# The head of an adaLN attention and GLU block: modulation weights in two pieces, K and Q passes interleaved, LayerNorm divided differently, planner constants refitted

## The chip, the cores and the metric

One core of a Trainium2 chip runs the whole program. The metric is the device time of one execution in microseconds. Before the change the median of 3 runs is 815.4 us (813.98 to 816.16). A profiled execution is recorded beside these runs; its span, from the program's first to its last recorded work, is 812.1 us. Engines are named as the profile names them: PE (TensorE, matrix products), PEld (its weight loads), DVE (VectorE), ACT (ScalarE), POOL (GpSimd), SP (SyncE, which here only issues DMAs).

## What is computed

```python
mod = silu(c) @ w_mod                      # 6 vectors of 640: sa, ca, ga, sb, cb, gb
h = layernorm(x) * (1 + ca) + sa           # x: 2048 x 640
q, k, v = split(h @ wqkv)                  # 32 heads of 20
p = softmax(q @ k.T * 20**-0.5)            # per head 2048 x 2048
x = x + ga * ((p @ v) @ wo)
h = layernorm(x) * (1 + cb) + sb
x = x + gb * (((h @ w_gate) * (h @ w_up)) @ w_down)   # 640 -> 1536 -> 640
```

All inputs and outputs are bf16. The largest piece of elementwise work is the softmax's exponential over 32 x 2048 x 2048 scores.

## The kernel before

**A planner in Python.** The kernel does not write its instruction order by hand. Each operation is a `Task` (L34) with an engine, a planned duration, dependences and a priority; `Sched` (L118) simulates the engines and lays tasks out in a fixed order for each engine, and `emit_program` (L322) writes that order with semaphore waits. At run time each engine works its list strictly in order: an instruction that waits holds all behind it on the same engine. `steal` (L272) lets the planner give an evacuation (a copy out of PSUM) that was meant for DVE to ACT. The constants at the top steer the plan: `QUADS` (L433), `HEADG` (L440), `LN_ACT` (L496), `GATE_F`, `STAGE` (L511 to 549, overrides by item) and others.

**Head.** One DMA each brings c (SP queue), token tiles 0 and 1 of x (`x00`, SP) and tiles 2 and 3 (`x01`, ACT queue), modulation vector 0 (`wm0`, sa, SP) and vector 1 (`wm1`, ca, ACT queue), each of 640x640 (`load_wm`, L801). The SP queue then waits for the first LayerNorm instruction (`ln_mark`) and issues the first half of wk, x of token chunk 1, the first half of wq, and so on (`load_rest`). A token chunk has 512 tokens, four tiles of 128. `col_round` (L927) multiplies one modulation vector's weights with silu(c), 25 matmuls per vector, into columns that an operation on DVE puts into `mcol`. `ln1` (L965) normalizes the four tiles of a chunk: by BN_STATS on DVE (L1012 to L1021), or, for tiles in `LN_ACT`, by two passes on ACT with accumulation (L975, L978); both with a power on POOL (L1021) and a normalization on DVE. `hT_rounds` (L1047) transposes the normalized tiles on PE, 128x128 each, by feature block of 128 columns (L1068, four tiles for each block), and evacuates each block with the modulation applied (ACT L1074, DVE L1076), after both modulation vectors. `kq_round` (L1102) then computes 4 heads of K (20 matmuls, L1107, evacuated by L1120/L1121), and of Q (L1127/L1128); `packed_round` (L1165) does so for other heads; `v_round` (L1248) computes V in quarter tiles (L911, L1260/L1261). Where PE has nothing, `do_fill` (L2343) issues matmuls without use (L2355 and L2357) that keep it active. `SCb` (L1344) and `load_wm(3/4)` (L1340) prepare the other modulation vectors.

**Attention.** The scores are computed transposed in PSUM, in units of 128 keys x 512 columns (L1448). Most units are exponentiated on ACT (L1484, into PP), in groups of 2 units (128x1024); from group `HEADG` on groups of 3 (128x1536) alternate with groups of 2. Some sets of four units, `QUADS` of them in each item, go to DVE instead, which forms the exponential with integer operations (L1508 into DB, then L1540, L1545, L1548 into DSS). PE multiplies both with V (L2005). The 40 items are 5 query chunks (512, 512, 512, 256, 256 rows) times 8 sets of 4 heads. The rest of the work (wo, the second LayerNorm, the GLU and w_down) of a chunk is spread over the items of the next.

**Tail.** What is left when the last exponential ends: the last PV products, wo, LayerNorm 2 (transposes L1763, evacuation h2Tc L1770 on ACT) and the GLU of the last 256 rows (L907, L911), and the output DMA.

Of the kernel before, what the change touches and what calls it, by code (L numbers as in the profile page):

```python
# [27 lines left out]
STEAL_END = 66197.894  # L28
STEAL_GAP = 200
# [292 lines left out]
def emit_program(nc, sched, nsem_dma=56):  # L322
# [83 lines left out]
    with nc.Block() as block:  # L406
# [20 lines left out]
        def _(e):  # L427
# [5 lines left out]
QUADS = ((0, 4, 3, 3, 3, 3, 4, 4),  # L433
# [6 lines left out]
HEADG = 580  # L440
# [5 lines left out]
LN2T = 0.6  # L446
# [4 lines left out]
XBACK = 1  # L451
# [3 lines left out]
TPRIO = 0.75  # L455
# [4 lines left out]
HEAD_OUT = 2  # L460
NPS = 4
TS_4X, TT_2X = 600.0, 1145.0
WM_GATE = 9
# [9 lines left out]
PVMIN, PVMAX, PVCAP = 2, 7, 13  # L473
PV0 = 0
V_PARTS = [[0, 4], [4, 8]]
V_L1 = 0.2
TAILX = 1
PASSDEP = 0
# [3 lines left out]
PASS_TC = (0, 1, 2, 3)  # L482
HT0_SPLIT = 0
PREEMPT = 0.0
PRE_M = 0.3
PV0N = 1
GATE_F = (0.468, 0.693, 0.969, 0.732, 1.0)
# [8 lines left out]
LN_ACT = [1, 3, 5, 7]  # L496
# [4 lines left out]
HT_L = 0.25  # L501
V_L = 0.221
LATE_A = 2.065
LATE_L = 1.418
LATEQ = (3,)
LATEQ_A = 2
# [6 lines left out]
    1: {"HOLD": 91, "D_LATE": 10, "PVMAX": 7},  # L513
    2: {"DL": 0.376, "D_LATE": 17},
    3: {"STEAL_GAP": 200, "PVMAX": 5, "FILL_MIN": 4781.051, "X_LATE": 38.763},
    5: {"EAGER": 7, "D_RES": 27, "PVCAP": 8},
    6: {"PVCAP": 12, "FILL_MIN": 4102.43, "D_LATE": 12, "PVMIN": 2},
    7: {"DL": 0.501, "PVCAP": 8, "PVTOL": 347},
    10: {"PVMAX": 8, "X_LATE": -27.967, "EAGER": 11, "D_LATE": 9},
    11: {"EAGER": 11, "DL": 0.443, "X_LATE": -8.435, "FILL_MIN": 4364.854, "PVTOL": 245, "HOLD": 134, "PVMAX": 9, "PVCAP": 13},  # L520
    12: {"FILL_MIN": 4969.105, "D_LATE": 7, "STEAL_GAP": 194.93, "X_LATE": -138.337, "DL": 0.459},
    13: {"DL": 0.417, "D_RES": 10, "HOLD": 84, "PVMAX": 6},
    14: {"D_LATE": 14, "D_RES": 22, "FILL_MIN": 4272.896, "EAGER": 10, "X_LATE": -52.696, "STEAL_GAP": 200},
    15: {"X_LATE": -15.741, "FILL_MIN": 4338.164, "HOLD": 175, "EAGER": 13},
    16: {"FILL_MIN": 3909.78, "D_RES": 55, "HOLD": 133, "PVCAP": 11},
    17: {"DL": 0.465, "D_LATE": 17, "PVMAX": 9, "PVMIN": 2, "STEAL_GAP": 195.663},
    18: {"FILL_MIN": 4326.704, "D_RES": 10},
    19: {"D_LATE": 18, "DL": 0.471, "FILL_MIN": 3976.707},
    20: {"DL": 0.391, "D_LATE": 14, "PVCAP": 13, "FILL_MIN": 5000},
    21: {"D_RES": 10, "PVCAP": 20, "HOLD": 96, "PVMAX": 6, "PVMIN": 2, "D_LATE": 19},  # L530
    22: {"PVMAX": 7, "FILL_MIN": 3913.503, "D_RES": 17, "X_LATE": -76.434, "EAGER": 6, "D_LATE": 16, "PVCAP": 13},
    23: {"PVTOL": 247, "PVMAX": 7, "D_RES": 23},
    24: {"PVCAP": 13, "PVMAX": 7, "PVMIN": 2, "FILL_MIN": 4085.526, "DL": 0.464, "EAGER": 7, "STEAL_GAP": 200, "HOLD": 231},
    25: {"STEAL_GAP": 200, "HOLD": 144, "X_LATE": 22.894, "D_RES": 10, "FILL_MIN": 4068.834, "DL": 0.549, "PVCAP": 15, "D_LATE": 14},
    26: {"D_RES": 15, "X_LATE": -39.384, "PVMAX": 9, "PVCAP": 14, "STEAL_GAP": 200, "DL": 0.411},
    27: {"DL": 0.473, "D_LATE": 6, "PVMAX": 6, "EAGER": 6, "D_RES": 75, "PVTOL": 249, "PVMIN": 2, "X_LATE": -47.659},
    28: {"PVCAP": 13, "HOLD": 166, "X_LATE": 82.94},
    29: {"PVCAP": 14, "EAGER": 5, "PVMAX": 7, "D_RES": 46},
    30: {"X_LATE": -110.495, "PVCAP": 15, "FILL_MIN": 3782.61, "D_LATE": 16, "PVTOL": 292},
    31: {"D_RES": 19, "FILL_MIN": 4905.173, "D_LATE": 15, "PVMIN": 2, "X_LATE": 36.868},  # L540
    32: {"PVMIN": 2, "D_LATE": 17, "D_RES": 78},
    33: {"STEAL_GAP": 199.702, "D_LATE": 18, "PVCAP": 14, "PVMAX": 4, "DL": 0.442, "PVTOL": 353, "D_RES": 17, "PVMIN": 2, "HOLD": 100},
    34: {"X_LATE": 150, "D_LATE": 22, "HOLD": 117},
    35: {"PVMIN": 2, "PVMAX": 8, "FILL_MIN": 4516.564, "STEAL_GAP": 179.748, "X_LATE": -53.091, "HOLD": 151, "D_LATE": 12, "PVCAP": 14},
    36: {"PVMIN": 2, "D_RES": 10, "DL": 0.524, "X_LATE": -6.364, "FILL_MIN": 4156.61, "PVMAX": 8, "HOLD": 33},
    37: {"D_LATE": 12, "PVTOL": 254, "PVCAP": 13, "FILL_MIN": 4699.279},
    38: {"D_RES": 60, "PVMAX": 7, "PVTOL": 450, "HOLD": 67, "D_LATE": 16},
    39: {"FILL_MIN": 3000, "D_LATE": 17, "PVTOL": 258, "X_LATE": -54.236, "PVCAP": 16},
}
XHALF = 1  # L550
STG_G0, STG_G, XC_G = 12, -10, -20
X_LATE = -24.052
# [11 lines left out]
def build_kernel(nc, A_x, A_wqkv, A_wo, B_x, B_w_gate, B_w_up, B_w_down, c, w_mod, out):  # L564
# [70 lines left out]
    mcol = alloc("mcol", [128, 4, KD], F32)  # L635
    st = alloc("st", [128, 4, 12], F32)
# [177 lines left out]
    load_wm(0, wm_a[0], "sp", 0.3)  # L814
    load_wm(1, wm_a[1], "act", 0.4)
    for t, land in ((d_x[0][0], 5000.0), (d_x[0][1], 4100.0), (d_wm[0][0], 9400.0), (d_wm[1][0], 8000.0)):
        t.land = land
    chained = [d_x[0][0], d_x[0][1], d_wm[1][0], d_wm[0][0]]

    def chain(f, *a):  # L820
        deps = [ln_mark[0]]
        tot = 0
        for t in reversed(chained[4:]):
            if tot >= DMA_WINDOW:
                deps = [t]
                break
            tot += t.nbytes
        f(*a, deps)
        return deps

    def load_rest():
        chain(load_w, d_wk, 0, 1, wk_sb, 0, "sp", 0.5)
        chained.append(d_wk[0])
        first2 = [lambda: chain(load_x, 1, 0, "sp", 0.6), lambda: chain(load_w, d_wq, 0, 0, wq_sb, 0, "sp", 0.55 if WQ_FIRST else 0.7)]
        if WQ_FIRST:
            first2.reverse()
        for q, f in enumerate((first2[0], first2[1],
# [126 lines left out]

    def ln1(tc, prio):  # L965
# [3 lines left out]
        for i in range(4):  # L969
            t = tc * 4 + i  # L970
            if t in LN_ACT:
                jx = xn[:, s2, i, :]
                tiny = (lambda f_, d_: dve(75, f_, d_, prio=prio + .1 * i)) if tc < 2 else (
# [6 lines left out]
                if i == 0 and tc == 0:  # L980
# [3 lines left out]
                p2 = pool(570, lambda e, t=t: e.tensor_tensor(rs[:, t:t + 1], sd[:, t:t + 1], mhalf[:, 0:1], ALU.pow),  # L984
                          [q4, p_mh], prio=prio)
# [25 lines left out]
            for hf in range(2):  # L1011
                bns.append(dve(393, lambda e, t=t, i=i, hf=hf: e.bn_stats(  # L1012
                    st[:, i, 6 * hf:6 * hf + 6], x0[:, t, 320 * hf:320 * hf + 320]),
                    [d_x[tc][i // 2], ag_prev.get(i)], prio=prio + .1 * i))
                if t == 0:
                    ln_mark[:] = bns[-1:]
            ag = dve(75, lambda e, t=t, i=i: e.bn_aggr(mv[:, t, :], st[:, i, :]), bns, prio=prio + .1 * i)
            ag_prev[i] = ag
            f1 = lambda e, t=t: e.tensor_scalar(sd[:, t:t + 1], mv[:, t, 1:2], EPS, None, op0=ALU.add)
            p1 = dve(75, f1, [ag], prio=prio + .1 * i) if tc < 2 else pool(220, f1, [ag], prio=prio)  # L1020
            p2 = pool(570, lambda e, t=t: e.tensor_tensor(rs[:, t:t + 1], sd[:, t:t + 1], mhalf[:, 0:1], ALU.pow),  # L1021
                      [p1, p_mh], prio=prio)
            f = lambda e, t=t, i=i: e.tensor_scalar(
# [3 lines left out]
            else:  # L1027
                t_xn[tc].append(dvl(360, f, [p2] + dps, prio=prio + .05 + .1 * i))

    t_hT = {}  # L1030

    def hT_rounds(tc, prio):
# [3 lines left out]
        if tc == 0 and HT0_SPLIT:  # L1036
            bs = [{} for _ in range(KD)]
            prev = None
            for i in range(4):
                for k in range(KD):  # L1040
# [4 lines left out]
                    if i == 0:  # L1045
# [9 lines left out]
                    if i == 3:  # L1055
# [46 lines left out]
    def kq_round(kind, j, tc, prio, gate=0):  # L1102
# [50 lines left out]
        elif tc not in LATEQ:  # L1153
            proj_early.append(r.last)
# [1278 lines left out]
```

## Time and profile before

| what | value |
|---|---|
| median of 3 runs | 815.4 us (813.98 to 816.16) |
| span of the profiled execution | 812.1 us |
| granted PE clock, mean | 1.00 |
| exponentials on ACT (L1484) | 677 of 128x1024 (mean 1126 ns), 98 of 128x1536 (mean 1546 ns) |
| units on DVE (L1508) | 400 (mean 680 ns), 100 chains of DSS operations (705, 688, 1224 ns) |
| first exponential starts | 15.90 us |
| ninth exponential starts | 26.67 us |
| last exponential ends | 779.23 us |
| fill matmuls | 23 of 128x512, 300 of the 32-column kind |

How to read the lines shown below. In the list of groups each line gives a line of the kernel, engine, operation, output and inputs, shapes, the count, busy time in us, mean ns of one, and the idle time of the engine just before them, with what ended it. In the list of waits: who waited for whom, the total in us, how often, and the longest. In the busy time by stage: the stretch, its length, then busy us of PE, PEld, DVE, ACT and POOL with instruction counts, the granted PE clock, the DMA share and GB/s. In the chain and the timeline: start, duration in us, and what ran.

### The profile page before, as it was taken

The numbers are of one execution on the slowest core, as the hardware profiler recorded it, in microseconds if no ns is written. First come the engines' busy times: TensorE is split into PE (matmuls) and PEld (weight loads), VectorE is DVE, ScalarE is ACT, GpSimd is POOL, SyncE is SP. The second block draws the span as 40 slices with busy tenths as digits, with TensorE's granted clock in tenths as the row PEclk, the third lists the DMA queues.
The fourth block names the chain that finished last, engine by engine and source line by source line (L and its number), as shares of the span: only waits on it lengthen the run. The fifth ranks groups of instructions, "written<-read, shape, count | busy, mean of one in ns | idle before, by whom it ended". The sixth has DMA issues, their size and how long they took to land.

```text
span 812.1 us, 28878 instructions
## 1 busy us (share of the span) xinstructions
PE 784.0 (97%) x12493; PEld 305.3 (38%) x12493; DVE 719.8 (89%) x1275; ACT 773.8 (95%) x818; POOL 79.1 (10%) x105
## 2 busy tenths in 40 slices
PE   9999999999999999999999999999889999999998
PEld 4433333322233223233233322233244444554567
DVE  7989999899999999999999999998999886667753
ACT  7899999999999999999999999999999999999942
POOL 3300000020002000000011000000011000001000
DMA  9624211214330244000400222000400146105610
GB/s 314 204 84 105 69 46 37 52 29 124 95 68 25 52 104 134 23 11 22 93 6 6 55 48 61 6 18 23 87 8 22 39 95 139 36 30 130 142 37 17
DMA packets 116445, 54.71 MB, mean 67 GB/s; under 512 B 83915, under 2 KB 116319, under 8 KB 116319
## 3 DMA queue, kind: packets, MB, share of 16 engines
q1 hardware_dynamic: 115391, 51.72, 24.6%
q8 instruction: 99, 1.62, 0.8%
q10 hardware_dynamic: 928, 1.15, 0.4%
q14 instruction: 27, 0.22, 0.1%
HBM read 41.85 MB, written 8.41 MB: 62 GB/s over the span
## 4 chain that ended last, share of the span: by engine, by line
PE 40%; ACT 37%; DVE 15%; issue 7%; DMA 1%; ACTq 0%; DVEq 0%
ACT PP L1484 37%; PE ps_all L911 12%; PE ps_all L1448 12%; PE ps_all L2005 9%; DVE DB L1508 5%; PE ps_all L907 3%; DVE DSS L1545 2%; DVE DSS L1548 2%; DVE DSS L1540 1%; PE ps_all L1171 1%; PE ps_all L1107 1%; DMA wm<-in_w_mod_dram 1%; PE ps_all L1068 1%; DVE wd L1434 1%; DVE gsb L1852 1%
## 5 line engine op out<-in xcount | busy, mean ns | idle before, releaser
L1484 ACT ACTIVATE PP<-ps_all 128x1024 bf16<-128x1024 f32 (+1 forms) x775 | 754.7, 1179 | 4.4 <-PE ps_all L1448 3.0
L1448 PE MATMUL ps_all<-QT,KT 32*128 32x512 bf16 (+1 forms) x2560 | 308.1, 340 | 18.1 <-ACT PP L1484 12.4
L1508 DVE TENSOR_SCALAR DB<-ps_all 128x512 int16<-128x512 f32 x400 | 264.4, 680 | 35.7 <-PE ps_all L1448 34.7
L1448 PEld LDWEIGHTS ps_all<-QT,KT 32*128 32x128 bf16 x2560 | 81.3, 91 | 262.7 <-ACT PP L1484 235.3
L2005 PE MATMUL ps_all<-PP,Vf 128*32 128x512 bf16 (+2 forms) x2084 | 164.2, 343 | 0.4 <-DVE OT L1632 0.4
L1545 DVE TENSOR_TENSOR DSS<-DB,DSS 128x2048 bf16<-128x2048 bf16 x100 | 122.4, 1224 | 0.0
L911 PE MATMUL ps_all<-h2T,stg 128*32 128x512 bf16 (+1 forms) x1740 | 115.9, 345 | 0.9 <-DVE DB L1508 0.2
L1638 POOL TENSOR_TENSOR OTn<-OT,invT 128x512 bf16<-128x512 f32 (+1 forms) x39 | 46.6, 1195 | 598.9 <-DVE invT L1636 598.9
L2005 PEld LDWEIGHTS ps_all<-PP,Vf 128*32 128x32 bf16 (+1 forms) x2084 | 45.9, 93 | 87.5 <-issue 79.8
L2005 PE MATMUL ps_all<-DSS,Vf 128*32 128x512 bf16 (+3 forms) x952 | 77.3, 349 | 0.9 <-DVE DSS L1545 0.5
L1540 DVE TENSOR_SCALAR DSS<-DB 128x2048 int16<-128x2048 int16 x100 | 70.5, 705 | 0.8
L1548 DVE TENSOR_SCALAR DSS<-DB 128x2048 int16<-128x2048 int16 x100 | 68.8, 688 | 0.3 <-PE ps_all L2005 0.3
L911 PE MATMUL ps_all<-wd,hprod 128*32 128x320 bf16 (+1 forms) x1316 | 58.5, 284 | 0.1
L911 PEld LDWEIGHTS ps_all<-h2T,stg 128*32 128x32 bf16 x1740 | 38.9, 95 | 34.6 <-issue 17.6
L911 PEld LDWEIGHTS ps_all<-wd,hprod 128*32 128x32 bf16 x1316 | 31.2, 96 | 16.6 <-issue 7.4
L2005 PEld LDWEIGHTS ps_all<-DSS,Vf 128*32 128x32 bf16 (+1 forms) x952 | 23.9, 95 | 24.4 <-issue 14.1
L911 PE MATMUL ps_all<-wV,hT 128*32 128x320 bf16 (+1 forms) x704 | 32.3, 289 | 0.1
L1171 PE MATMUL ps_all<-hT,wq 128*32 128x512 bf16 x375 | 31.6, 382 | 0.1
L911 PE MATMUL ps_all<-wo,Ocp 128*32 128x320 bf16 (+1 forms) x628 | 28.2, 286 | 0.3
L2357 PE MATMUL ps_all<-ident 128*32 128x512 bf16 x300 | 27.0, 383 | 0.3 <-DVE DB L1508 0.2
L1852 DVE CAST gsb<-ps_all 128x512 bf16<-128x512 f32 x36 | 24.4, 678 | 3.0 <-PE ps_all L911 3.0
L1632 DVE STREAM_TRANSPOSE OT<-ps_all 128x512 f32<-128x512 f32 (+1 forms) x40 | 24.1, 602 | 2.8 <-PE ps_all L2005 2.7
(122 smaller groups left out, 507.0 us busy)
## 6 DMA issues: line engine op xcount, KB each, us to landing
stg<-in_B_w_gate_dram SPq DMA_DIRECT2D x50, 160.0 KB
stg<-in_B_w_up_dram SPq DMA_DIRECT2D x50, 160.0 KB
QT<-q_rows SPq DMA_DIRECT2D x22, 128.0 KB
KT<-k_rows SPq DMA_DIRECT2D x84, 32.0 KB
wm<-in_w_mod_dram SPq DMA_DIRECT2D x3, 800.0 KB
x<-in_A_x_dram SPq DMA_DIRECT2D x7, 320.0 KB
xck<-in_A_x_dram SPq DMA_DIRECT2D x3, 640.0 KB
wd<-in_B_w_down_dram SPq DMA_DIRECT2D x1, 1920.0 KB
```

Of the source, the lines that this page charges most:

```text
L911: return lambda e, b: e.matmul(ps[32 * x:32 * x + 32, b, c0 + o:c0 + o + w], lhs()[:, 32 * x:32 * x + 32], rhs() if w == n else rhs()[:, o ...
L1171: f = [lambda e, b_, k=k, x=x: e.matmul(ps[x:x + min(32, w - x), b_, :], wx[:, k, r0 + x:r0 + min(x + 32, w)], hT[tc][:, k, :], tile_posit ...
L1448: ems.append(lambda e, i=i, kt=kt: e.matmul(dstf()[:, i * u.n:(i + 1) * u.n], KT[32 * u.s:32 * u.s + 32, u.j, kt * 128:(kt + 1) * 128], QT ...
L1484: return e.activation(PPs[g % 2][:, cellp["p"], 0:nu * 512], ps[:, b0:b0 + nu, :].rearrange("p b c -> p (b c)"), AFT.Exp, scale=ESCALE)
L1508: return e.tensor_scalar(DB0[:, st_["slot"], x * 512:(x + 1) * 512], bank(cell["b"]), EBIAS, 0.0, op0=ALU.add, op1=ALU.max)
L1540: return e.tensor_scalar(DSS[:, st_["ss"][0], :], DB0[:, st_["slot"], :], 0x7F, 0x3F00, op0=ALU.bitwise_and, op1=ALU.bitwise_or)
L1545: return e.tensor_tensor(d, DB0[:, st_["slot"], :].bitcast(BF16), d, ALU.mult)
L1548: return e.tensor_scalar(DSS[:, st_["ss"][1], :], DB0[:, st_["slot"], :], 0x7F80, 2, op0=ALU.bitwise_and, op1=ALU.bitwise_or)
L1638: f3 = lambda e: e.tensor_tensor(OTn[:, 0:n].rearrange("p (b c r) -> p b r c", c=32, r=2), OT[:, 0:n].rearrange("p (b r c) -> p b r c", c= ...
L1852: f = lambda e: e.tensor_copy(gsb[:, gs, 0:n], ps[:, r.b["b"], 0:n])
L2005: ems.append(lambda e, i=i, kt=kt, stt=stt, stp=stp: e.matmul(ps[32 * s:32 * s + mc, BPV, 0:u.n], Vf[:, (kt * H + 4 * u.j + s) * VW:(kt * ...
L2357: task.emits = [lambda e, x=x: e.matmul(ps[32 * x:32 * x + 32, b_, :].rearrange("p (a b) -> p a b", a=4), ident[:, 32 * x:32 * x + 32], id ...
```

## The change

1. **Modulation weights in two pieces** (`WMP`). Vectors 0 and 1 are each loaded as feature blocks 0 to 2 (128x5x384) and 3 to 4 (128x5x256). The SP queue's order becomes c, x00, first piece of vector 0, wk, second piece of vector 1, second piece of vector 0, wq, then (after `ln_mark`) x of chunk 1; the ACT queue has x01 and the first piece of vector 1. The columns are computed by piece (30 and 20 matmuls), with one DVE operation for both vectors, and an hT evacuation waits for its block's piece alone. 
2. **Transposes of chunk 0 by token tile** (`HT0_SPLIT`, `HT_ORD`): all five blocks of tile 2, then of tiles 0, 3, 1. On PE they stand between the column matmuls.
3. **K and Q interleaved** (`kq_first`): for each feature block k, 4 matmuls of K on the first 256 tokens and 4 of Q on 512; each k waits only for its block of hT. Q's evacuation is in two halves. K of the other 256 tokens follows later (20 matmuls), in the planned order behind the second 4-head set's K and the first two score groups.
4. **LayerNorm** (`LN_ACT`): tiles 3 and 5 on ACT (before 1, 3, 5, 7), tiles 1 and 7 on DVE; one power on POOL serves tiles 1 and 3; small steps of chunk 0 get an earlier priority.
5. **Constants refitted**: most of the planner's, among them `QUADS` (items 4 and 10 and 31 one quad more on DVE, item 11 one less), `HEADG` 580 to 590, `STEAL_END`, `GATE_F`, priorities and `STAGE`.

In the instruction order that the planner now gives: 682 exponentials of 1024 and 92 of 1536; 408 units on DVE; 17 and 292 fills; after the first exponential ACT has LayerNorm's second pass for tile 5, and after the eighth three hT evacuations of chunk 1, one of packed Q (KPA), one of KT and one of Vf before the ninth. In the tail 48 of the hprodt matmuls stand behind the last transposes.

```diff
-QUADS = ((0, 4, 3, 3, 3, 3, 4, 4),
-         (3, 4, 2, 4, 3, 4, 4, 4),
+QUADS = ((0, 4, 3, 3, 4, 3, 4, 4),
+         (3, 4, 3, 3, 3, 4, 4, 4),
          (3, 3, 4, 4, 3, 4, 4, 4),
-         (1, 2, 1, 2, 2, 1, 1, 1),
+         (1, 2, 1, 2, 2, 1, 1, 2),
          (1, 1, 1, 1, 1, 1, 1, 1))
-HEADG = 580
+HEADG = 590
...
-PASSDEP = 0
+PASSDEP = 1
...
-PASS_TC = (0, 1, 2, 3)
-HT0_SPLIT = 0
+PASS_TC = (0,)
+WMP = ((0, 3), (3, 5))
+H_LAND = (5000.0, 4100.0, 6300.0, 6700.0, 7800.0, 8500.0, 9300.0, 10400.0)
+HT_ORD = (2, 0, 3, 1)
+LNP1, LNP2, LNP3 = 3.0, 3.9797, 5.0
+HT0_SPLIT = 1
...
-LN_ACT = [1, 3, 5, 7]
+LN_ACT = [3, 5]
...
-    load_wm(0, wm_a[0], "sp", 0.3)
-    load_wm(1, wm_a[1], "act", 0.4)
...
+    def load_wp(pi, v, eng, prio):
+        a_, z_ = WMP[pi]
+        d_wp[(pi, v)] = dma(eng, 128 * KD * 128 * (z_ - a_) * 2, lambda e: e.dma_start(
+            wm_a[v][:, :, a_ * 128:z_ * 128], wmv[:, :, v * D + a_ * 128:v * D + z_ * 128]), prio=prio, dur=550.0)
+        return d_wp[(pi, v)]
+
+    chained = [d_x[0][0], d_x[0][1], load_wp(0, 1, "act", .3), load_wp(0, 0, "sp", .3)]
+    load_w(d_wk, 0, 1, wk_sb, 0, "sp", .35)
+    chained += [d_wk[0], load_wp(1, 1, "sp", .4), load_wp(1, 0, "sp", .45)]
+    load_w(d_wq, 0, 0, wq_sb, 0, "sp", .5)
...
-    r_sa = col_round(0, 0, 1, False)
-    r_ca = col_round(1, 1, 2, True)
-    ev_col = [r_sa.evac[0], r_ca.evac[0]]
+    def col_piece(pi):
+        a_, z_ = WMP[pi]
+        w_ = z_ - a_
+        mms = []
+        for v in (1, 0):
+            for nbk in range(a_, z_):
+                for k in range(KD):
...
+        def after(r):
+            f = lambda e: e.tensor_tensor(mcol[:, 0:2, a_:z_], ps[:, r.b["b"], 0:2 * w_].rearrange("p (v k) -> p v k", v=2),
+                                          mone[:, :, a_:z_], ALU.add)
+            return [dve(75, f, [r.last] + d_m1, prio=0)]
...
-            for i in range(4):
+            for ii, i in enumerate(HT_ORD):
                 for k in range(KD):
...
-                        ev = evac(512, 455, f, fa, [t] + ev_col)
+                        ev = evac(512, 455, f, fa, [t, ev_k[k]])
...
+    def kq_first():
...
+        for k in range(KD):
+            for wx, c_, n in ((wk_sb, kb, 256), (wq_sb, qb, 512)):
+                f = [lambda e, wx=wx, c_=c_, n=n, k=k, s=s: e.matmul(
+                    ps[32 * s:32 * s + 32, c_["b"], 0:n], wx[:, k, DH * s:DH * s + 32], hT[0][:, k, 0:n],
+                    tile_position=(0, 32 * s), start=(k == 0), stop=(k == KD - 1), skip_group_check=True) for s in range(4)]
+                dps = (hd + w_deps("K", 0) if k == 0 else list(pd[k])) if wx is wk_sb else w_deps("Q", 0) if k == 0 else []
...
+        r = Round(mms, [lq], after, 12, name="K0.0b")
+        kt_ready[(0, 0)] = [ek, r.evac[0]]
...
-            kq_round("K", 0, 0, 11)
-            kq_round("Q", 0, 0, 12)
+            kq_first()
```

The constants that are left out above (`GATE_F`, `STAGE` and the like) are numbers in the same places.

More of the change, by code (lines that the diff above doesn't have):

```diff
@@ L831, in load_rest @@
     def load_rest():
[L832 to L837, printed above, removed]
+        for q, f in enumerate((lambda: chain(load_x, 1, 0, "sp", 0.6),
                                lambda: chain(load_x, 1, 1, "sp", 0.8), lambda: chain(load_w, d_wv, 0, 2, wV, 0, "sp", 0.9),
@@ L968, in ln1 @@
         t_xn[tc] = []
-        for i in range(4):
+        for i in (0, 1, 3, 2) if tc == 0 else range(4):
             t = tc * 4 + i
```

220 lines of the change are left out of this document (151 added, 69 removed).

## The prediction

> **What bounds the kernel now.** I read the page's busy line first, then the costliest groups, then the waits.
>
> ```profile
> PE 784.0 (97%) x12493; PEld 305.3 (38%) x12493; DVE 719.8 (89%) x1275; ACT 773.8 (95%) x818; POOL 79.1 (10%) x105
> ...
> L1484 ACT ACTIVATE PP<-ps_all 128x1024 bf16<-128x1024 f32 (+1 forms) x775 | 754.7, 1179 | 4.4 <-PE ps_all L1448 3.0
> ```
> ```profile
> PEld ps_all L1448 <- ACT PP L1484: 235.3, 660, 1.0
> ...
> ACT PP L1484 <- PE ps_all L1448: 3.0, 6, 1.3
> ```
>
> Three engines look full, but the waits choose: TensorE's weight loads for scores wait 235.3 us for ScalarE's exponentials, which wait 3.0 us for scores. ScalarE sets the pace. The busy time by stage says where:
>
> ```profile
> 0.00:16.00 16.00, 14.04 (x175) 6.84 (x179) 11.76 (x48) 10.28 (x23) 4.79 (x14) 1.00 0.95 322
> 16.00:60.00 44.00, 43.87 (x712) 19.29 (x704) 39.25 (x89) 39.65 (x46) 9.54 (x22) 1.00 0.54 160
> ...
> 320.00:528.00 208.00, 203.09 (x2857) 64.86 (x2855) 205.23 (x334) 207.64 (x227) 17.46 (x17) 1.00 0.15 35
> ...
> 779.00:812.00 33.00, 29.18 (x377) 23.31 (x369) 15.55 (x41) 6.17 (x16) 1.29 (x2) 1.00 0.06 22
> ```
>
> The fourth time is ScalarE: 39.65 of 44 us in the ramp, full to 779, idle in the tail. So the time is four terms: the first exponential's start (15.90), ScalarE's work and gaps in the ramp, the sum of exponentials, and the tail from the last one's end (779.23) to 812.1. By shapes the trace has 677 exponentials of 128x1024 and 98 of 128x1536. Their mean durations (1126, 1546 ns) overlap; start to start, back to back, they take 0.904 and 1.331 us: 742.4 in all.
>
> The head's chain, in order of time, is one line of TensorE work behind a DMA:
>
> ```profile
> 1.17 6.34 DMA wm<-in_w_mod_dram
> 7.56 0.78 PE ps_all L932 x25
> 8.34 0.67 PE ps_all L2355 x3
> 9.01 0.66 PE ps_all L932 x25
> 9.67 1.23 PE ps_all L1068 x20
> 10.90 0.86 PE ps_all L2355 x4
> 11.77 3.42 PE ps_all L1107 x60
> 15.19 0.33 PE ps_all L1448 x4
> ```
>
> From 3 us on the DMA engines are full (some 0.39 MB each us), so order and bytes decide when weights land. ScalarE's next gap is the important one:
>
> ```profile
> 15.90 7.40 ACT L1484 ACTIVATE PP<-ps_all 128x1024 bf16<-128x1024 f32 x8
> 23.25 0.43 ACT L1261 CAST Vf<-ps_all 128x320 bf16<-128x320 f32 x1
> 24.33 0.69 ACT L1128 ACTIVATE QT<-ps_all,qcol 128x512 bf16<-128x512 f32 x1 [0.65 <-PE ps_all L1107]
> 25.41 0.59 ACT L1121 CAST KT<-ps_all 128x512 bf16<-128x512 f32 x1 [0.39 <-PE ps_all L1107]
> 26.09 0.43 ACT L1261 CAST Vf<-ps_all 128x320 bf16<-128x320 f32 x1
> 26.67 1.02 ACT L1484 ACTIVATE PP<-ps_all 128x1024 bf16<-128x1024 f32 x1 [0.16 <-PE ps_all L1448]
> ```
>
> The ninth exponential starts at 26.67, 10.77 after the first; eight need 7.23, so this gap costs 3.54: three evacuations and the waits between. Later ones, after exponentials 15, 23, 35 and 39, cost 1.5, 1.5, 1.5 and 0.8.
>
> **The first exponential.** The last piece of modulation weights (vector 0, blocks 3 and 4) now has 2.70 MB ahead of its end: 0.66 of x, 1.64 of both vectors, 0.41 of wk, which goes first. Before it was 2.29 MB, without wk. The trace had moved 2.29 MB by 8.2 us and vector 0's columns could start by 9.01; it had moved 2.70 by 9.3, so, with the same delay of 0.5 to 0.8, 9.8 to 10.1. But rows are cut from 1280 bytes to 768 and 512. The trace has no such loads; its nearest are 640-byte rows, at 0.36 MB/us against 0.396 for 1280. At 0.36 the 1.64 MB take 0.4 more: 10.2 to 10.5. I take 10.1, between.
>
> [...]
>
> Behind the last piece TensorE, in its new order, has 10 column matmuls (10 of 25 in 0.78: 0.3), 5 transposes of tile 3 (0.3) and a fill (0.22) before the last 5 transposes, of tile 1, at P = 10.9. LayerNorm of tile 1, now on VectorE (x landed at 4.96; six statistics 0.38 to 0.41 apart, small steps, three powers of 0.59 on POOL, one behind tile 3's second ScalarE pass, three normalizations 0.36 apart), ends by 9.9 to 10.35: hidden by half a microsecond. Then: five hT evacuations (three on DVE 0.45 apart, two on ScalarE) with the interleaved pass of K (half width) and Q behind them, end at P+2.5; 20 K matmuls of the second weight block (1.08, row L1107), P+3.6; VectorE's one K and two Q copies of 256 columns (0.41 each) lie beside it; scores at P+3.7; ScalarE's K copy (0.59) to P+4.4; the exponential at P+4.45 = 15.35. I keep 14.8 to 15.9: **0.55 earlier** (0 to 1.1).
>
> The SP queue puts the second token chunk's x behind both last pieces and wq: 3.44 MB instead of 3.03, so some 1.1 us later, 11.9 instead of 10.8 by the same curve. Behind it waits, on ScalarE, tile 5's first LayerNorm pass (0.74+0.19), and behind that the K copy. That pass cannot begin before the two hT evacuations end (P+1.9 = 12.8) and is over 0.8 us before the K copy can start (14.5): 0. If x came after 13.5, each microsecond would delay the first exponential by one. wq (3.11 MB, 11.0 to 11.4) is wanted at 11.5.
>
> **The ninth exponential.** TensorE's order now has, between the eighth and ninth score pairs, the second token chunk's last transposes, a packed Q pass and a K pass (20 matmuls each, 1.08). Before, transposes lay among the score pairs, and Q took the place of packed Q. On ScalarE, LayerNorm's second pass (0.83+0.19 = 1.02) moved behind the first exponential, and three hT evacuations (two of them, 1.45 at 0.69 to 0.77 each, ahead of these passes) came in. Sum from the first exponential: 7.23+1.02, evacuations 1.45, packed Q 1.08, K 1.08, release 0.25, K copy 0.6 and 0.05, score to exponential 0.43: 13.2, against 10.77. Start 28.5 against 26.67: **1.9 later** with 15.35. If VectorE, which works from P+2.5 without a pause to the second chunk's LayerNorm, has those tiles earlier than the eighth exponential, part of the evacuations goes between exponentials: bounds 0.8 earlier (same 10.77, start 15.1) and 2.3 later. I take 1.6, nearest to the summed rows.
>
> From there TensorE's order is nearly that of before, for some twenty score pairs; the gaps of 1.5, 1.5, 1.5 and 0.8 stay: 0, bounds -0.5 and +0.5.
>
> **The exponentials.** The new order has 682 of 1024 and 92 of 1536: 5 x 0.904 - 6 x 1.331 = **-3.5 us**. Their 8 units of 512 columns (and two chains more) go to VectorE: 8 x 0.68 + 2 x (0.705 + 0.688 + 1.224) = 10.7 us, beside exponentials where VectorE has room. At the change's two added quads, items 4 and 10 (111 to 135 and 254 to 278 us, if an item takes 64 of 2048 units), VectorE was busy 23.28 and 22.57 of 24 us. A quad taken out at item 11 gives one back, and the one added at item 31 falls where VectorE is a quarter idle. So I count 0 beyond the 3.5, bounds -2 and +3. Below nothing too: outside the ramp some 11 us of small gaps lie in the exponentials' row, and the new constants may trim them.
>
> **The tail.** 48 matmuls of 128x320 (wd, hprodt; 140 took 4.87, so 1.67) now stand behind the last chunk's transposes, in a place where TensorE waited 1.1 us for h2Tc: **+0.5**, bounds 0 and 1.7. Fewer fills (17 wide for 23, 292 for 300) cost nothing while other work fills TensorE: the granted clock was 1.00 in every stage.
>
> **Sum:** +1.6 (which contains the 0.55) - 3.5 + 0.5 = -1.4 us. On the profiled execution's 812.1 that is 810.7. The median of 815.4 lies 3.3 above its span, taken as unchanged: **814.0**.
>
> **Rivals.**
> - *Balance pays in full* (faster). The second chunk's LayerNorm ends early enough that the ninth exponential still comes 10.8 after the first: -0.8 - 3.5 + 0.5 = -3.8, 811.6; with gaps trimmed by 2, 809.6. For it: ScalarE's gaps of 0.65 and 0.39 there were waits for TensorE, so evacuations may fill waits. Against: VectorE's queue, and TensorE's order puts two passes behind the last evacuation.
> - *VectorE becomes the bound* (slower). Each added quad is 5.35 us; item 10 has 1.4 to spare, item 4 has 0.7. Where VectorE's units hold PSUM banks longer, score pairs come late and ScalarE waits. If half of each excess reaches ScalarE: (3.9 + 4.6)/2 = 4.3, so +2.9, 818.3. It decides from an excess of 1.4 us reaching ScalarE, where the gain is gone. For it: 205.23 of 208 busy from 320 to 528. Against: score matmuls and their weight loads waited for those units' VectorE rows only 6.8 us in all.
> - *The change doesn't do what it says.* The last piece lands at 10.5 or later, wq behind it at 11.4 or later, and the first exponential is no earlier than 15.9: 0.55 more, -0.9, 814.5. It hardly differs from the forecast in time.
>
> **How the numbers follow.** Forecast 0.42 (own range 812.5 to 816.5), the no-earlier-head case 0.08, full balance 0.31, VectorE bound 0.19. 0.3% of 815.4 is 2.4 us, about what a measurement can tell from no change: faster is below 813.0, which takes the full balance and 0.07 of the forecast: 0.38. Slower is above 817.8: 0.15 of the VectorE case and 0.05 of the forecast with its bounds against it: 0.20. The rest, 0.42, is within. The range leaves out some 0.1 at each end: 809.6 to 818.3.
>
> **What would show it.** The first exponential at 14.8 to 15.9 and the ninth near 28.3; the fence above with hT evacuations on ScalarE between them; 774 exponentials, their idle time near 4.4 us; VectorE's busy time up by 10 us; the last exponential's end to the end of the span 0.5 longer. I am wrong if the ninth comes before 27, if ScalarE's idle time grows by over 2 us near items 4 and 10, or if the K pass's start is set by a DMA other than the last modulation piece.

## The result, and the profile after

The changed kernel takes 817.5 us (median of 20 runs, 816.79 to 819.73) against 815.3 for the kernel before: ratio 1.003 (95% interval 1.0019 to 1.004), 2.2 us slower. 814.0 and a gain of 1.4 had been predicted; the time lies inside the range, on the other side of no change. That it lies inside is luck: the range's upper end, 818.3, is the price of the VectorE rival, which did not come true. The time of an execution of either kernel is its span and 1.75 to 1.9 us; the 3.3 that the prediction put around the span was wrong, because its profiled execution (812.1) was one at full clock, and the median is not.

Executions of both kernels differ above all by TensorE's granted clock, so spans are compared at equal clock where that is said (before, at granted clock 1.00: 812.1 to 813.1, most of them 812.1 to 812.3; in its series of 35 the 24 at 0.991 to 0.998 have 813.6 to 817.1).

The busy line and the clock by slices, from the page of the changed kernel:

```profile
PE 784.6 (96%) x12507; PEld 306.1 (37%) x12507; DVE 727.6 (89%) x1293; ACT 769.6 (94%) x813; POOL 75.7 (9%) x104
...
PEclk8999999999999999999999999999999999999999
```

ScalarE is busy 4.2 us less and VectorE 7.8 us more, where some 10 had been counted. New is the second line: the clock by slices, which the page of before did not have at all, shows 8 tenths in the first slice. The busy time by stage (stretch, its length, busy us of PE, PEld, DVE, ACT, POOL, granted clock, DMA share, GB/s):

```profile
0.00:16.00 16.00, 12.30 (x108) 5.77 (x112) 7.95 (x38) 5.60 (x11) 3.24 (x11) 0.82 0.97 288
16.00:60.00 44.00, 43.76 (x721) 19.26 (x709) 38.22 (x95) 38.82 (x47) 10.41 (x23) 0.99 0.57 173
```

In the first 16 us TensorE works 1.7 us less than before at 0.82 of its clock, and DMA brings 288 GB/s instead of 322. The head's chain, in order of time (start, duration, what):

```profile
3.31 8.05 DMA wm<-in_w_mod_dram
...
11.40 0.43 PE ps_all L979 x10
11.83 0.56 PE ps_all L1099 x5
12.39 0.43 PE ps_all L2470
...
14.63 2.72 PE ps_all L1221 x33
```

The last columns start at 11.40, where 10.1 was taken, and the fills and passes behind them have nearly twice the price that they have at full clock in the run warm below: a fill 0.43 for 0.22, the pass of K and Q 2.72 for 1.55. ScalarE's row from the first exponential on:

```profile
18.66 0.58 ACT L1179 CAST KT<-ps_all 128x512 bf16<-128x512 f32 x1 [3.43 <-PE ps_all L1165]
19.14 1.03 ACT L1599 ACTIVATE PP<-ps_all 128x1024 bf16<-128x1024 f32 x1
20.06 0.83 ACT L1017 ACTIVATE xn<-x,mv 128x640 bf16<-128x640 bf16 x1
...
20.87 6.50 ACT L1599 ACTIVATE PP<-ps_all 128x1024 bf16<-128x1024 f32 x7
27.19 2.23 ACT L1132 ACTIVATE hT<-ps_all,mcol 128x512 bf16<-128x512 bf16 x3
...
31.21 0.58 ACT L1179 CAST KT<-ps_all 128x512 bf16<-128x512 f32 x1 [0.48 <-PE ps_all L1165]
```

The first exponential starts at 19.14 (before 15.90), the ninth at 32.47 (26.67). The two profiled executions compare so, in us:

| term | before | after | difference | predicted |
|---|---|---|---|---|
| first exponential starts | 15.90 | 19.14 | +3.2 | -0.55 |
| from there to the ninth | 10.78 | 13.32 | +2.5 | +2.15 |
| ninth to the last one's end | 752.55 | 749.88 | -2.7 | -3.5 |
| from there to the end | 32.83 | 34.01 | +1.2 | +0.5 |
| span | 812.06 | 816.37 | +4.3 | -1.4 |

### The profile page after: what moved, and what is told of

It reads as the page before. It is cut to its first block, busy times and chain, and to the rows that moved or that the text cites. A ratio compares the mean times of both kernels' runs of the same rounds, so it can differ in the third digit from the quotient of the medians.

```text
span 816.4 us, 28941 instructions
## 1 busy us (share of the span) xinstructions
PE 784.6 (96%) x12507; PEld 306.1 (37%) x12507; DVE 727.6 (89%) x1293; ACT 769.6 (94%) x813; POOL 75.7 (9%) x104
## 4 chain that ended last, share of the span: by engine, by line
ACT 47%; PE 34%; issue 10%; DVE 8%; DMA 1%; SPq 0%; ACTq 0%; DVEq 0%
ACT PP L1599 47%; PE ps_all L1563 11%; PE ps_all L925 9%; PE ps_all L2120 7%; PE ps_all L921 3%; DVE DB L1623 2%; PE ps_all L1287 2%; DMA wm<-in_w_mod_dram 1%; DVE DSS L1660 1%; DVE DSS L1655 1%; PE ps_all L1165 1%; DVE DSS L1663 1%; DVE wd L1549 1%; DVE st L1059 1%; PE ps_all L1126 0%
## 5 line engine op out<-in xcount | busy, mean ns | idle before, releaser
L1623 DVE TENSOR_SCALAR DB<-ps_all 128x512 int16<-128x512 f32 x408 | 271.5, 682 | 31.4 <-PE ps_all L1563 30.5
L1660 DVE TENSOR_TENSOR DSS<-DB,DSS 128x2048 bf16<-128x2048 bf16 x102 | 125.2, 1227 | 0.0
L1753 POOL TENSOR_TENSOR OTn<-OT,invT 128x512 bf16<-128x512 f32 (+1 forms) x39 | 44.3, 1137 | 602.0 <-DVE invT L1751 602.0
L2120 PE MATMUL ps_all<-DSS,Vf 128*32 128x512 bf16 (+1 forms) x976 | 78.0, 348 | 0.2
L1655 DVE TENSOR_SCALAR DSS<-DB 128x2048 int16<-128x2048 int16 x102 | 72.2, 708 | 0.7
L1663 DVE TENSOR_SCALAR DSS<-DB 128x2048 int16<-128x2048 int16 x102 | 70.6, 692 | 0.3 <-PE ps_all L2120 0.3
L2120 PEld LDWEIGHTS ps_all<-DSS,Vf 128*32 128x32 bf16 x976 | 24.9, 95 | 19.8 <-issue 10.5
L925 PE MATMUL ps_all<-wo,Ocp 128*32 128x320 bf16 (+1 forms) x652 | 30.2, 282 | 0.6 <-DVE DB L1623 0.3
L2472 PE MATMUL ps_all<-ident 128*32 128x512 bf16 x292 | 25.1, 383 | 0.3 <-DVE DB L1623 0.2
```

The lines of the kernel that those rows point to most:

```text
L925: return lambda e, b: e.matmul(ps[32 * x:32 * x + 32, b, c0 + o:c0 + o + w], lhs()[:, 32 * x:32 * x + 32], rhs() if w == n else rhs()[:, o ...
L1623: return e.tensor_scalar(DB0[:, st_["slot"], x * 512:(x + 1) * 512], bank(cell["b"]), EBIAS, 0.0, op0=ALU.add, op1=ALU.max)
L1655: return e.tensor_scalar(DSS[:, st_["ss"][0], :], DB0[:, st_["slot"], :], 0x7F, 0x3F00, op0=ALU.bitwise_and, op1=ALU.bitwise_or)
L1660: return e.tensor_tensor(d, DB0[:, st_["slot"], :].bitcast(BF16), d, ALU.mult)
L1663: return e.tensor_scalar(DSS[:, st_["ss"][1], :], DB0[:, st_["slot"], :], 0x7F80, 2, op0=ALU.bitwise_and, op1=ALU.bitwise_or)
L1753: f3 = lambda e: e.tensor_tensor(OTn[:, 0:n].rearrange("p (b c r) -> p b r c", c=32, r=2), OT[:, 0:n].rearrange("p (b r c) -> p b r c", c= ...
```

## The experiments

Theory at the start: the loss is the head's, by late transfers and the halved clock. Rivals: an accident of one execution; the first exponential late by the DMA alone; the exponentials' order.

**again.** No edit.

> The changed kernel once more, unaltered. Theory: two things together make the head late, (1) the last piece of modulation weights lands at 11.4 us because rows of 512 and 768 bytes move slowly (0.29 to 0.33 MB/us after 5 us), and (2) TensorE then waits and its granted clock falls to 0.5 from 10.1 to 17.0 us. Both belong to the program, so both are there again: first exponential at 18.5 to 19.5 us, clock 0.5 in most of 10 to 17. Rival: the slow transfers were an accident of that one execution (wk's 640-byte rows too moved at 0.30 there against 0.36 before); then the last piece lands at 10.2 to 10.6, the clock stays at 1.00 and the first exponential comes at 15.3 to 16.5.

Median 818.3; span 816.8. Second pieces' columns at 10.25 and 11.38, clock 0.5 from 9.3 to 16.2, first exponential at 18.73: it belongs to the program. The clock falls at window borders that lie differently in each execution (10.14 us in the changed kernel's, 9.34 in again, 8.33 in fills, 9.78 in mone_last). The windows of the changed kernel's own execution:

```profile
6.73:10.14 3.41, 1.73 (x41) 1.45 (x41) 2.60 (x13) 0.09 (x1) 1.25 (x2) 1.00 1.15 301
10.14:13.55 3.41, 3.02 (x33) 1.98 (x34) 0.75 (x3) 0.48 (x1) 0.00 (x0) 0.50 1.12 330
```

In the first, TensorE is busy 1.73 of 3.41 us, with no idle stretch over 1.30; in the second the clock is 0.50. In the execution again, 2.13 of 3.41 were followed by the same. So here the clock fell behind windows that were half busy or more. Busy time alone doesn't give a threshold: in before_shift and before_quads the clock fell far from the head (at 622 and 579 us) behind 3.41 us with TensorE busy 2.80 and 2.96, while the changed kernel had 3.41 us with 2.55 busy near 587 us and kept its clock at 1.00.

**fills, warm.** More fills where TensorE waits, orders unchanged; first the edit of fills.

```diff
+    hf = [t for t in sc.order["pe"] if t.name == "fill"]
+    hf[11].emits = hf[11].emits * 8
+    hf[12].emits = hf[12].emits * 3
```

> The changed kernel with nine more fill matmuls (128x512) where TensorE waits for the second pieces: the one ahead of tile 0's transposes eight times, the one between the two vectors' columns three times; all orders else as they are. Theory: the clock falls because TensorE stands idle some 1.5 us of the window from 6.7 to 10.1; with the fills it stays at 1.00, and then the transposes, the K and Q passes and the scores go at full speed: the last transposes start at about 12.2, the first exponential at 16.5 to 16.9 instead of 19.1, and the time is 1.5 to 2.5 us less than the changed kernel's. Rival: the first exponential is late from the DMA alone (TensorE would only wait elsewhere): it stays within 0.5 us of 19.1, and the time doesn't move.

Median 817.0. The first exponential moved to 18.11 only: the clock fell earlier, from 8.3 to 11.7, after a window with TensorE busy 1.98 us, so that eight fills took 3.57 us. Neither the theory's number nor the rival's held, and it led to warm:

```diff
+    for i_, n_ in ((10, 6), (11, 6), (12, 3)):
+        hf[i_].emits = hf[i_].emits * n_
```

> The changed kernel with twelve more fills (128x512), spread otherwise than before: the last of the six after c's transpose six times, the one ahead of tile 0's transposes six times, the one between the columns three times. In the run with fills in one place the granted clock fell earlier, from 8.3 to 11.7 us, because TensorE had stood idle from 5.8 to 7.3. Theory: idle time in any window of 3.4 us between 5 and 11.4 halves the clock; with both gaps filled the clock stays at 1.00 up to 20 us, the last columns start at 11.4 as the DMA allows, the last transposes at 12.2 to 12.4, the first exponential at 16.5 to 17.0, and the time falls by 2 to 2.5 us against the changed kernel. Rival: the short matmuls and transposes don't keep the clock up whatever fills stand between; then it falls again in some window before 17 and the first exponential stays above 17.5.

Median 815.77, ratio to before 1.0006 (0.9995 to 1.0018); against the changed kernel's 817.5 and 818.3 that is 1.7 to 2.5 us. Clock 1.00 throughout the head, first exponential at 16.61. From warm's chain:

```profile
11.41 0.40 PE ps_all L979 x10
...
12.11 0.22 PE ps_all L2470
12.33 0.28 PE ps_all L1099 x5
...
13.26 1.55 PE ps_all L1221 x36
```

The columns start as late as before the edit (11.41), and what follows has its full-clock price. So the halved clock costs 2.5 us of the first exponential's delay (19.14 to 16.61) and, by the medians, most of the measured loss. Something else varies too: two of the changed kernel's 20 timed executions had granted clock 1.00 and yet spans of 815.2 and 815.3. No trace of them is kept. Warm's own profiled execution, 815.0 at clock 1.00 where most are 813.8 to 814.0, has a tail 1.2 us longer than the changed kernel's; whether those two are the same case is not shown. The last transposes start at 12.33 and the first exponential 4.3 later; the prediction had 4.45.

**whole_rows.** Whole vectors at the first pieces' places, wk ahead.

```diff
-            wm_a[v][:, :, a_ * 128:z_ * 128], wmv[:, :, v * D + a_ * 128:v * D + z_ * 128]), prio=prio, dur=550.0)
+            *((wm_a[v][:, :, :], wmv[:, :, v * D:(v + 1) * D]) if pi == 0 else
+              (dum[:, v, :], wmv[:, 0, v * D:v * D + 64]))), prio=prio, dur=550.0)
...
+    o_.insert(o_.index(d_wp[(0, 0)]), d_wk[0])
```

> The changed kernel with its orders on all engines, but both modulation vectors loaded whole (rows of 1280 bytes) at the place of their first pieces, wk ahead of vector 0 on the SP queue, and two loads of 128 bytes by 128 partitions in place of the second pieces, so that TensorE waits at the same places. The bytes ahead of the last columns are those of the changed kernel (2.70 MB). Theory: the cut rows cost the time; the last columns can start at 9.8 to 10.4 instead of 11.4, and the first exponential comes 1 us earlier or more (up to 3.5 if the clock stays at 1.00). Rival: the bytes ahead or the queue's order cost it, not the rows; then the last columns start at 11 or later again.

Median 819.2; the last columns start at 13.02. That isn't when their weights came:

```profile
10.78 0.56 PE L981 MATMUL ps_all<-scol,wm 128*128 128x1 bf16 x15 [2.52 <-DMA wm<-in_w_mod_dram]
...
13.02 0.45 PE L981 MATMUL ps_all<-scol,wm 128*128 128x1 bf16 x10
```

TensorE waits 2.52 us, until 10.78, for vector 0, which here comes whole, and then works without a wait to 13.02, at half clock. So uncut rows brought the last weights 0.6 us earlier (10.78 for 11.40), not the 1.0 to 1.6 of the theory, and the time didn't gain. Packets of 1280 bytes took 60 ns from 5 us on (55 before) and 640 bytes 35 to 38 (32): 3 to 6 ns more at both lengths.

**paced.** Waits on SP only.

```diff
+    for t_, d_ in ((d_wp[(1, 1)], d_x[0][0]), (d_wp[(1, 0)], d_wp[(0, 0)]), (d_wq[0], d_wk[0]),
+                   (d_x[1][0], d_wp[(1, 1)]), (d_wv[0], d_wp[(1, 0)])):
+        t_.deps = list(t_.deps) + [d_]
```

> The changed kernel with waits on the SP queue alone: the second piece of vector 1 is issued when x00 has landed, that of vector 0 when its first piece has, wq after wk, x of chunk 1 and wV after the second pieces; never more than some 1900 rows stand in the queue. In the changed kernel the SP queue was held in issuing from 2.7 to 9.3 us, and from 5.0 us every packet took 4 to 6 ns longer than packets of the same size before (640 bytes 38 ns for 32, 1280 bytes 60 for 55). Theory: a queue that is kept full slows the packets; paced, 640-byte rows go at 32 ns again and the last columns start at 10.2 to 10.6 instead of 11.4. Rival: the slowness comes from something else that begins at 5 us; then packets of 640 bytes still take 37 to 38 ns and the columns start at 11.2 or later.

Median 818.0, columns at 11.42, 640-byte packets 38 ns at 7 us: the full queue was not it.

**stats_first.** BN_STATS and aggregations of chunk 1 ahead of the first K copy, on VectorE alone.

```diff
+    i_ = sc.all.index(k_ev[0])
+    sc.all[i_:i_] = mv_
```

> The changed kernel with the six BN_STATS and three aggregations of chunk 1 moved, on VectorE alone, from behind the first K and Q copies to ahead of them, where VectorE stood idle from 14.4 to 17.4 us. Theory: from the first to the ninth exponential (13.3 us) the time is VectorE's queue as well as ScalarE's: with 2.9 us of statistics gone from it the second chunk's transposes no longer wait, but ScalarE's three hT evacuations still stand behind the eighth exponential, so the ninth comes 0.3 to 0.8 us earlier. Rival: only the sum of evacuations and passes behind the eighth exponential counts: 13.3 as before; or VectorE is the only bound: 2 us or more earlier.

Median 818.0; 13.28 between first and ninth exponential for 13.32. The rival's "13.3 as before" held.

**landings.** One constant, everything planned anew.

```diff
-H_LAND = (5000.0, 4100.0, 6300.0, 6700.0, 7800.0, 8500.0, 9300.0, 10400.0)
+H_LAND = (5400.0, 4300.0, 7400.0, 7900.0, 9300.0, 10700.0, 11850.0, 12600.0)
```

> The changed kernel with one line changed: the landing times that its planner assumes for the first eight DMAs are set to those that the trace shows (second pieces 10.7 and 11.85 us on the planner's clock instead of 8.5 and 9.3, first pieces 7.4 and 7.9 instead of 6.3 and 6.7, wq 12.6 for 10.4), and everything is planned anew. The plan now puts all transposes and more fills ahead of the second pieces' columns, chunk 1's statistics ahead of the K copy, and chunk 1's transposes among the score pairs. Theory: the assumed landings, not the idea of the change, cost the time: the clock stays up, the first exponential comes at 15.2 to 16.2, the ninth 10.5 to 11.5 later, and the time is 3 to 5 us below the changed kernel's, at or under the kernel before (-0.5 to -2.5). Rival: with second pieces at 11.4 the head can't be as fast as before (first exponential after 16.5), or planning anew loses outside the head what it gains: no better than the kernel before.

Median 832.8. Half and half: the clock stays up in the head, 10.74 us from the first to the ninth exponential (as before the change), but the first only at 16.97; and outside the head the new plan loses 15 us (ninth to last 765.1 for 749.9). Of these, 6.7 us arise (against the changed kernel's exponentials, counted one by one) from 630.1 to 647.2, where TensorE's clock is halved in five windows on end; the other 8.5 lie elsewhere. The constants that were refitted fit one plan.

**before_quads.** The other side of that.

```diff
-         (3, 4, 2, 4, 3, 4, 4, 4),
+         (3, 4, 3, 3, 3, 4, 4, 4),
...
-HEADG = 580
+HEADG = 590
```

> The kernel before with the changed kernel's QUADS and HEADG alone, head and all other constants as before. Theory: outside the head the change gains (682 and 92 exponentials instead of 677 and 98, 3.5 us less, of which some 2.7 arrived between the ninth exponential and the last), so this kernel is 1.5 to 3.5 us faster than the kernel before. Rival: the gain there comes with the other refitted constants, and these two edits alone make gaps: same or slower.

Median 821.7, ratio 1.0085 (1.0054 to 1.0116): the rival. The same 682 and 92 exponentials, yet 754.5 us from the ninth to the last for before's 752.6 (with one halved window in it, at 579 us), and 4.2 more in the tail. The gain in the exponentials comes only with the other constants.

**square_early, square_stats, whole_first.** All with warm's fills. ScalarE's second pass of tile 5 ahead of the K copy; then also tile 4's statistics; then also whole vectors ahead of wk.

```diff
+                if t == 5:
+                    ln_early.extend([q1, q2, q3])
...
+            if t == 4:
+                ln_early.extend(bns + [ag])
...
+    i_ = sc.all.index(k_ev[0])
+    sc.all[i_:i_] = ln_early
```

> The run with twelve fills (clock kept up; 13.33 us from the first to the ninth exponential), with tile 5's LayerNorm passes moved: the second one (1.02 us on ScalarE) from behind the first exponential to ahead of the K copy, where ScalarE stood idle, and the small VectorE step that it needs ahead of the first K copy. Theory now: two chains of equal length end together at the ninth exponential, ScalarE's (second pass, eight exponentials, three hT evacuations) and VectorE's (statistics, copies, normalizations, up to the bank that chunk 1's transposes wait for); shortening VectorE's alone gave 0.05. Then shortening ScalarE's alone gives little too: the ninth exponential comes 0 to 0.4 earlier at an unchanged first one (12.9 to 13.3 after it). Rival: ScalarE's sum alone sets it, as the prediction had it: 12.3 after the first one, and 1 us less in the time.

815.9; 13.27 from the first to the ninth exponential: taking 1.02 us from ScalarE there gave 0.06.

> The run before this one, with tile 4's two BN_STATS and its aggregation on VectorE also moved ahead of the first K copy (0.9 us), so that both chains are shorter. Theory of two equal chains: now the ninth exponential comes 0.7 to 1.0 earlier than with the fills alone (12.3 to 12.6 after the first), and the time is 0.5 to 1.0 us below theirs. Rival, neither chain but TensorE's order of passes: 13.3 as before.

815.6; 13.13. Both together gave 0.2, not 0.7. What was left is TensorE: by the chain of this arrangement (read in mone_last_all, below) it works without a pause from the first scores to the ninth pair's. So three chains end nearly together there; that TensorE's is the third is read from the chain, no run shortened it.

> The same, with both modulation vectors loaded whole and ahead of wk (two loads of 128 by 128 bytes stand for the second pieces, then wk, wq). Theory: the place of the last columns sets the first exponential one for one until LayerNorm of tile 1 (10.1) does; the last columns start at 9.0 to 9.8 instead of 11.4, the last transposes at 10.1 to 10.7, the first exponential at 14.6 to 15.4 instead of 16.6, the ninth at 26.9 to 27.9, and the span at full clock is 811 to 812.5, at or below the kernel before (812.1). Rival: packets stay slow from 5 us on as in every kernel with the new order of loads, and wk and wq now come too late: first exponential after 15.8, no gain over the fills.

816.6, first exponential at 17.66, 1280-byte packets 60 ns from 5 us: the rival's numbers, but not by its mechanism. TensorE's row, with L2480 the fills and L981 the columns:

```profile
9.51 0.53 PE L981 MATMUL ps_all<-scol,wm 128*128 128x1 bf16 x15 [0.90 <-DMA wm<-in_w_mod_dram]
...
10.01 1.46 PE L2480 MATMUL ps_all<-ident 128*128 128x512 bf16 x6
...
11.58 0.39 PE L981 MATMUL ps_all<-scol,wm 128*128 128x1 bf16 x10
11.83 0.81 PE L2480 MATMUL ps_all<-ident 128*128 128x512 bf16 x3
12.48 0.39 PE L981 MATMUL ps_all<-scol,wm 128*128 128x1 bf16 x10
```

All of vector 0 is there at 9.51, 1.9 us before the changed kernel's last piece. Then TensorE works without a wait, 2.3 us of it on fills that had been placed for waits which this order of loads no longer has. So the run doesn't tell what whole vectors ahead of wk are worth; no run here does.

**before_wk_early, before_wq_early.** The kernel before, wk (and wq) issued behind vector 0.

```diff
+    d_wk[0].deps = []
+    sc.all.remove(d_wk[0])
+    sc.all.insert(sc.all.index(d_wm[0][0]) + 1, d_wk[0])
```

> The kernel before with one edit: wk is issued on the SP queue right behind vector 0 (at about 2.1 us) and doesn't wait for the first LayerNorm instruction (it was issued at 6.1). Theory: a third large load that stands in the SP queue from the start is what slows packets from 5 us on; then 1280-byte packets take 60 ns instead of 55 from 5 us, and vector 0's columns start 0.3 to 0.7 later (9.2 to 9.6). Rival: packets are slow only where rows of different length are mixed or cut; then 55 ns as before, and nothing moves.

> The kernel before with wk and wq both issued right behind vector 0, so that the SP queue holds 2176 rows at 3 us (before, 896 until 6 us). Theory of the full queue: 1280-byte packets take 60 ns from 5 us on and vector 0's columns start at 9.2 or later. Rival, the address: 55 ns.

814.5 and 815.5 (ratios 1.0002 and 0.9997, both intervals about 1): packets 55 and 32 ns, columns at 8.89 and 9.00, first exponentials at 15.90 and 16.43. Not the early issue either.

**mone_last, before_shift.** The address, from both sides: the first edit is to the changed kernel, the second to the kernel before.

```diff
-    mone = alloc("mone", [128, 2, KD], F32)
     st = alloc("st", [128, 4, 12], F32)
...
     gs_off = region(2 * 512 * 2)
+    mone = alloc("mone", [128, 2, KD], F32)
```
```diff
+    pad = alloc("pad", [128, 10], F32)
     st = alloc("st", [128, 4, 12], F32)
```

> The changed kernel with one line moved: the table mone is allocated behind the other tiles, so that x, the modulation weights, wk and wq lie at the addresses of the kernel before. Theory of the address: packets of 640 bytes take 32 ns again and of 1280 bytes 55, the last columns start at 10.0 to 10.6 instead of 11.4, and the first exponential comes 1 us earlier or more. Rival: it is the queue or the cut rows; then 38 ns at 7 us and 11.4 as before, and the time doesn't move.

> The kernel before with an unused table of 64 bytes per partition at the place where the changed kernel has mone: all later tiles move by 64 bytes, all else is as before. Theory of the address: packets of 1280 bytes take 60 ns from 5 us on and of 640 bytes 35 to 38, vector 0's columns start at 9.3 to 9.7 instead of 8.9, the time rises by 0.3 to 1 us. Rival: 55 and 32 ns as before.

Packets and columns came as the theory said. With mone last, packets of 640 bytes take 32 ns, of 768 36 (41), of 512 27 (32); the last columns start at 10.52. With an unused table in the kernel before, which takes 64 bytes, 1280-byte packets take 60 ns from 5 us on, the columns start at 9.37 for 8.89 and the first exponential at 16.29 for 15.90. The stages of the changed kernel and then of mone_last, last column GB/s:

```profile
5.00:7.00 2.00, 1.61 (x4) 0.30 (x2) 2.00 (x12) 1.13 (x3) 0.55 (x1) 1.00 1.11 327
7.00:9.00 2.00, 1.73 (x41) 1.45 (x41) 1.53 (x9) 0.00 (x0) 1.02 (x2) 1.00 1.15 303
```
```profile
5.00:7.00 2.00, 1.55 (x4) 0.30 (x2) 2.00 (x12) 1.13 (x3) 0.55 (x1) 1.00 1.09 368
7.00:9.00 2.00, 1.73 (x41) 1.45 (x41) 1.53 (x9) 0.00 (x0) 1.02 (x2) 1.00 1.15 342
```

The same instructions in the same order, and 13% more bytes. Median 817.0, which is 0.5 to 1.3 us under the changed kernel's two medians; the clock still fell in this kernel (0.5 from 9.8 to 13.2). The time of before_shift (814.9, ratio 1.0, 0.9981 to 1.0019) cannot tell 0.4 us from nothing; its trace can, and at clock 1.00 its six spans have a median of 812.7, before's eleven 812.2.

**mone_last_all.** mone last, warm's fills, square_stats' moves.

> The changed kernel with mone behind the other tiles, the twelve fills, and tile 5's second LayerNorm pass and tile 4's statistics moved to the idle places ahead of the first exponential (the run square_stats: span 813.7). Theory of the address: the last columns start at 10.0 to 10.6, the first exponential at 15.3 to 15.9, the ninth at 28.4 to 29.0, the span is 812.3 to 812.9, level with the kernel before at full clock (812.2), and the time is up to 1 us under its median, since the clock stays up. Rival: no gain over square_stats.

815.25, ratio to before 0.9991 (0.9977 to 1.0005): level, with columns at 10.81 and the first exponential at 16.0. The columns wait here for the fills ahead of them (mone_last had 10.52). At full clock its spans are 812.9 to 813.8, with a median of 813.15, 0.95 over before's; its median time is no worse, since it lost the clock in 4 of 12 executions and before in 24 of 35. From its chain:

```profile
24.92 0.55 PE ps_all L1131 x8
25.48 1.25 PE ps_all L1295 x20
26.72 1.08 PE ps_all L1170 x20
27.80 0.95 PE ps_all L925 x28
28.75 0.33 PE ps_all L1571 x4
```

Each piece begins where the one ahead of it ends: from the first scores on TensorE has no wait to remove, only work ahead of the ninth pair's scores (L1571).

## Why the prediction was wrong, step by step

1. **"Fewer fills (17 wide for 23, 292 for 300) cost nothing while other work fills TensorE: the granted clock was 1.00 in every stage."** This step failed, and it is the largest single error. It took the clock of one execution of the old order for a constant. The change delays TensorE's last weights, thins its work ahead of them and takes six wide fills away, and the clock fell to half (0.50 from 10.14 to 16.97 us); which of the three weighs most was not separated. again, fills and warm: 2.5 us of the first exponential, 1.7 to 2.5 us of the time. It does not alone explain the sign: with the clock kept up, warm is level with before by the medians, and the account at full clock below is 1.8 us longer, where 1.4 shorter was forecast. These 3.2 us are in steps 2, 4, 5 and 6.
2. **The last piece at 10.1.** 11.40 measured. The bounds (10.2 to 10.5 by 640-byte rows) were sound for what they covered: with mone last it is 10.52, so cut rows and wk ahead cost what the upper bound said. The other 0.9 us is the address shift by a table of 40 bytes that takes 64, which no step looked at. Short rows do cost time here: unshifted, 512-byte packets move 0.33 MB/us (mone_last, 27 ns each) against 0.396 for 1280 bytes (before, 55 ns each).
3. **P to the first exponential, 4.45.** 4.3 in warm: right. Tile 1's LayerNorm was hidden, as said: it ends at 10.06.
4. **First to ninth exponential, 13.2.** 13.32, the same within 0.01 us in six other runs of this order: the size was right, and in part by luck. The sum adds ScalarE's work to TensorE's passes, as if that were the one path; taking 1.02 us of it away from ScalarE gave 0.06, and shortening VectorE's part too gave 0.2. What remains is TensorE's work, which the sum did not count up to there. The balance that pays in full (10.8) did not come.
5. **The exponentials, -3.5.** -2.7 arrived, so 0.8 came back between the exponentials; what made these gaps is open. The "0 beyond" was a guess; VectorE did not become the bound in this plan (idle before exponentials 4.2 us, before 4.4), while in before_quads the same exponentials lost.
6. **Tail, +0.5.** +1.2. The 48 matmuls cost 0.6, as worked out: 10 transposes at 0.67, then 1.75 for 48 matmuls, where the two pieces had been 0.23 and 1.49 of waiting. The other 0.6 is between the last VectorE operation and the last write's landing; no run looked into it.

Of the rivals, "the change doesn't do what it says" came true in its first half (last piece after 10.5, first exponential after 15.9). Its price of -0.9 left out step 1, and what steps 4 to 6 add. At full clock the account is: first exponential +0.7 and to the ninth +2.55 (warm's), middle -2.7 and tail +1.2 (the changed kernel's), together +1.8. Most spans agree with it (warm at full clock 813.8 to 814.0, before 812.1 to 812.3); warm's profiled execution, with its longer tail, is 1.0 us above these.

Open: why the shifted addresses slow packets only from 5 us on and not the first 1.0 MB. The price is about the same for packets of 512 bytes (32 ns for 27) and of 1280 (60 for 55). The trace holds no addresses, and what makes this price is not shown.

## What to carry to other kernels

When a change makes TensorE wait early, look at its busy time in each stretch of 3.4 us: 1.73 to 2.13 us busy came before the fall of the clock in the head in four executions here (the changed kernel 1.73, fills 1.98, mone_last 2.01, again 2.13), and fills in the waits gave it back (warm, 1.00). A fill is cheap only in a wait: in whole_first, where the weights came earlier, the same fills, 2.3 us of them, held the columns up. A new small table belongs behind the tiles that DMAs write, so that these keep their addresses (mone_last, the last columns at 10.52 for 11.40). A plan that was fitted as a whole doesn't split into gains: two constants alone lost 6 us, one corrected constant 15.

## What was not expected of the hardware

A shift of all tiles behind the new table by 64 bytes (320 in whole_rows and whole_first) made DMA packets some 5 ns longer by the median (60 for 55, 41 for 36, 38 for 32, 32 for 27), in each of the twelve profiles with shifted tiles, from 5 us to 10.5 (paced) or 12 and later. The halved clock came in windows of 3.41 us, one, two or (landings) five in a row, whose borders lay elsewhere in each execution (8.33, 9.34, 9.78 and 10.14 us in four of them). In the kernel before, too, 24 of 35 executions in one series had a granted clock of only 0.991 to 0.998, the shortest of these spans 1.4 to 2 us over those at full clock; and in five profiles of kernels run here the clock fell far from the head (at 175 and 178 us in stats_first and mone_last_all, 579 in before_quads, 622 in before_shift and 630 in landings), in before_shift and before_quads behind 3.41 us in which TensorE was busy 2.80 and 2.96 us. The windows at 175 and 178 made the exponentials behind them 1.4 us later than the changed kernel's.
